# An S4D convolution beside a gated unit: magnitude powers two at a time over five chunks, output stores of the first half from GpSimd, the last Fourier stage before the last down block

## The chip, the cores and the metric

The kernel runs on one core of a Trainium2 chip. The core has five engines that work side by side, each in the order of its own instruction list: TensorE (matrix products), VectorE, ScalarE, GpSimd and SyncE, which only issues transfers. The metric is the device time of one execution in microseconds (us), lower is better; of several runs the median counts.

## What is computed

The layer norm of one input goes into two branches, and both are added to the input. Branch A is a state space convolution: a kernel of 2048 taps is generated for each of 448 channels from 256 complex modes, and convolved by Fourier transforms. Branch B is a gated unit with 1792 hidden columns.

```python
def _A_ref(u, log_A_real, A_imag, C_real, C_imag, log_dt, D_skip):   # u: (1, 2048, 448), modes: (448, 256)
    dt = jnp.exp(log_dt)
    A = -jnp.exp(log_A_real) + 1j * A_imag
    C = (C_real + 1j * C_imag) * dt[:, None]
    P = jnp.exp((A * dt[:, None])[:, :, None] * pos[None, None, :])
    K = 2.0 * jnp.einsum("dn,dnl->dl", C, P).real
    y = jnp.fft.irfft(Uf * Kf[None, :, :], L2)[:, :, :L]             # Uf, Kf: rfft of u and K at 2L
    y = y.transpose(0, 2, 1)
    return y + u * D_skip[None, None, :]

def _B_ref(x, w_gate, w_up, w_down):                                 # (448, 1792), (448, 1792), (1792, 448)
    h = _sigmoid(x @ w_gate) * (x @ w_up)
    return h @ w_down

xn = _layernorm(x)
return x + _A_ref(xn, ...) + _B_ref(xn, ...)
```

## The kernel before

Two Python generators, `conv` (branch A) and `glu` (branch B), emit instructions in turns; the main loop always continues the one that is behind by its planned share of work. A scheduler then sets the order within each engine's list, with `hp` (raised priority) and `issue_after` (not before a named instruction) as hints. At run time each engine works through its list in order and waits for semaphores.

**Branch A, generator `kgen`.** The 448 channels are worked in 56 chunks of 8 channels, 7 groups of 8 chunks. Per chunk TensorE multiplies phases by a selector (`tr`, line 539), ScalarE turns them into sines and cosines `S` (lines 545 to 548), VectorE multiplies those with magnitudes `me` and `mf` into `Et` and `Ft` (lines 599 to 601), and TensorE contracts them into `ko` (line 613). `S` for the next chunk is made one chunk ahead (`ahead`). The magnitudes are made by GpSimd for two chunks at a time (`magnitudes`, lines 505 and 517) by repeated doubling: each step multiplies a filled part of the row by one power. ScalarE adds squares to `me` (`squares`, line 530). GpSimd waits with a block until VectorE has read the block two before it, since `me` has two buffers.

**The powers.** `powers` makes what the doubling multiplies by: twelve arrays `pm[:, j]` for a whole group. It holds each power minus one, and VectorE squares it in that form (line 453: (w + 2) w), ten times in a chain; ScalarE adds the one at the end (line 451 for the first power, line 456 for j = 1 to 5 and for j = 7 to 11). `pm` has two buffers, one per group in turn. The first group's powers are made before the loop; those of group g + 1 are emitted at chunk 4 of group g (line 588), the magnitudes that read them at chunk 6. ScalarE's additions stand after `sins[0]`, the last sine step emitted so far.

**Branch B, `glu`.** Two halves of 1024 tokens. Per block of 128 hidden columns `gate` makes products `gu` (line 706), a tanh, and `hf`, the product of gate and up (line 717); its rounded part `hh` and rest `hl` feed the down products `po` (line 819) that VectorE adds into `acc` (line 824). Products are in split precision, three per pair.

**The end.** `spectra` multiplies the spectra (`there`, `back`) for the column half h = 0, then h = 1; `last(h, m)` is the closing Fourier stage (line 960) for four token blocks, two in each half of the tokens, and VectorE adds its result (line 968). The sums of tokens 0 to 1023 are in `ac`, the rest in `accs[2]` and `accs[3]`. `H` is 224, half the columns. `out` stores four token blocks of one column half in four transfers, which go to SyncE, ScalarE and GpSimd in rotation (`outs`). In the last group of `glu` (`final`) the down blocks run (t, b) = (0, 0) to (1, 3); before (1, 2) stand `last(1, 0)` and `last(1, 2)`, behind (1, 3) `last(1, 4)` and `last(1, 6)`. The first column half of `accs[2 + t]` is stored when block t is done, the second at the very end.

## Time and profile before

| | us |
|---|---|
| median of three runs | 716.96 |
| lowest, highest | 716.56, 721.07 |
| the profiled execution | 717.89 |
| its span in the profile | 716.1 |
| mean granted TensorE clock | 0.98 of full |

All durations come from the one profiled execution. A row of a timeline gives start, duration, engine, line, operation, output and inputs, shapes and count, and in brackets how long the engine stood idle before it and for whom. Rows that follow each other are merged, and "x6" says how many. A row of the groups gives the count, then busy time and mean of one in ns, then idle time before. A row of the waits gives who waited for whom: total, times, longest. PEld is TensorE's loading of weights, which runs beside the products; SPq and ACTq are the sequencers of SyncE and ScalarE issuing transfers.

### The profile page before, as it was taken

The page shows a single profiled execution, that of the slowest core. Times are in us where ns is not written, and L with a number is a line of the kernel's source. Part 1 is how long each engine was busy: PE and PEld are TensorE (multiplying, and loading weights), DVE is VectorE, ACT ScalarE, POOL GpSimd, SP SyncE. Part 2 cuts the span into 40 slices and gives each one's busy share as a digit, 9 for nine tenths or more (in the row PEclk, how much of TensorE's full clock was granted, in tenths as well). Part 3 has the DMA queues.
Part 4 walks back from the last instruction along what each step waited for, and adds up shares of the span by engine and source line. Part 5 has one row for each costly group of instructions (what it writes and reads, how often), then busy time and mean ns, then how long its engine had stood idle before and what let it go on. Part 6 is the DMA issues. An engine that isn't in the chain of part 4 may idle for free.

```text
span 716.1 us, 19096 instructions
## 1 busy us (share of the span) xinstructions
PE 671.3 (94%) x7752; PEld 528.2 (74%) x7752; DVE 550.8 (77%) x766; ACT 428.7 (60%) x678; POOL 378.8 (53%) x431
## 2 busy tenths in 40 slices
PE   3898999999997998999999999999989999999995
PEld 2676888878876885656878778887867777776784
DVE  5899997599889889898588988987936555556543
ACT  3656974588687689996578778678643322313320
POOL 2101138556987978797368688598954002351002
PEclk9998999999999898999999999999999999999998
DMA  9947174464254444556933333242259988999645
GB/s 204 235 145 231 50 230 132 145 198 136 63 169 148 138 111 127 160 164 196 274 107 101 95 110 116 68 147 57 57 173 309 242 234 239 264 281 222 182 131 154
DMA packets 93991, 117.22 MB, mean 164 GB/s; under 512 B 12240, under 2 KB 77776, under 8 KB 93904
## 3 DMA queue, kind: packets, MB, share of 16 engines
q1 hardware_dynamic: 65904, 91.87, 45.6%
q10 hardware_dynamic: 25424, 18.24, 8.8%
q0 software_dynamic: 2576, 5.90, 2.9%
q8 instruction: 61, 1.00, 0.6%
q14 instruction: 26, 0.21, 0.1%
HBM read 72.13 MB, written 43.84 MB: 162 GB/s over the span
## 4 chain that ended last, share of the span: by engine, by line
PE 71%; DVE 13%; ACT 4%; issue 3%; SPq 3%; DMA 3%; POOL 1%; ACTq 0%; POOLq 0%; DVEq 0%
PE gu L706 29%; PE po L819 17%; PE sp L900 7%; PE ko L613 6%; PE pv L927 4%; PE tr L539 4%; SPq L489 2%; DVE Et L599 1%; PE gu L281 1%; DVE Ft L601 1%; DVE Et L600 1%; DMA acc<-in_A_u_dram 1%; DMA ph<-ph_d 1%; DVE pm L453 1%; DVE hl L724 1%
## 5 line engine op out<-in xcount | busy, mean ns | idle before, releaser
L517 POOL TENSOR_TENSOR me<-me,pm 128x32 f32<-128x32 f32 (+1 forms) x168 | 145.1, 864 | 67.6 <-DVE Et L600 56.8
L517 POOL TENSOR_TENSOR mf<-mf,pm 128x64 f32<-128x64 f32 (+1 forms) x112 | 121.3, 1083 | 6.1
L706 PE MATMUL gu<-xh,wh 128*128 128x512 f32 x336 | 100.5, 406 | 0.7 <-ACT xh L221 0.7
L706 PE MATMUL gu<-xh,wl 128*128 128x512 f32 x336 | 96.2, 393 | 0.0
L706 PE MATMUL gu<-xl,wh 128*128 128x512 f32 x336 | 96.1, 392 | 0.0
L600 DVE TENSOR_TENSOR Et<-me,S 128x1024 f32<-128x1024 f32 x56 | 79.7, 1423 | 14.4 <-ACT me L530 14.0
L599 DVE TENSOR_TENSOR Et<-me,S 128x1024 f32<-128x1024 f32 x56 | 79.1, 1414 | 14.3 <-ACT S L548 13.6
L819 PE MATMUL po<-dh,hh 128*128 128x448 f32 x224 | 85.0, 379 | 2.9 <-DVE hf L717 2.9
L601 DVE TENSOR_TENSOR Ft<-mf,S 128x1024 f32<-128x1024 f32 x56 | 80.1, 1430 | 6.5 <-PE ko L613 4.0
L819 PE MATMUL po<-dl,hh 128*128 128x448 f32 x224 | 83.1, 371 | 0.0
L819 PE MATMUL po<-dh,hl 128*128 128x448 f32 x224 | 81.8, 369 | 0.0
L545 ACT ACTIVATE S<-tr 128x1024 f32<-128x1024 f32 x56 | 57.9, 1034 | 37.8 <-PE tr L539 36.1
L613 PEld LDWEIGHTS ko<-Et,Ft 128*32 128x32 f32 x3584 | 55.5, 112 | 30.6 <-issue 13.6
L706 PEld LDWEIGHTS gu<-xh,wh 128*128 128x128 f32 x336 | 61.7, 191 | 19.8 <-issue 4.4
L613 PE MATMUL ko<-Et,Ft 128*32 128x64 f32 x3584 | 66.5, 224 | 9.4 <-DVE Ft L601 7.4
L722 ACT CAST hh<-hf 128x512 fp32r<-128x512 f32 x56 | 35.0, 625 | 65.6 <-DVE hf L717 58.3
L706 PEld LDWEIGHTS gu<-xh,wl 128*128 128x128 f32 x336 | 63.4, 189 | 14.4 <-DVE hf L717 0.7
L706 PEld LDWEIGHTS gu<-xl,wh 128*128 128x128 f32 x336 | 63.4, 189 | 13.5
L783 POOL TENSOR_TENSOR dl<-rd,dh 128x448 fp32r<-128x448 f32 x14 | 26.2, 1871 | 83.5 <-ACT dh L782 83.5
L548 ACT ACTIVATE S<-S,hpi 128x1024 f32<-128x1024 f32 x56 | 65.7, 1174 | 0.0
L824 DVE SCALAR_TENSOR_TENSOR acc<-po,acc 128x448 f32<-128x448 f32 x80 | 48.0, 615 | 21.1 <-PE po L819 21.0
L717 DVE SCALAR_TENSOR_TENSOR hf<-th,gu 128x512 f32<-128x512 f32 x56 | 38.0, 679 | 32.1 <-PE gu L706 24.5
(208 smaller groups left out, 1302.1 us busy)
## 6 DMA issues: line engine op xcount, KB each, us to landing
sk_d<-sk ACTq DMA_DIRECT2D x14, 512.0 KB
sx<-x_d SPq DMA_DIRECT2D x32, 224.0 KB
skl<-sk_d SPq DMA_DIRECT2D x16, 448.0 KB
vp<-v_d SPq DMA_DIRECT2D x16, 448.0 KB
v_d<-vt SPq DMA_DIRECT2D x14, 448.0 KB
ph<-ph_d SPq DMA_DIRECT2D x224, 24.0 KB
wt_d<-wh SPq DMA_DIRECT2D x9, 512.0 KB
wt_d<-wl SPq DMA_DIRECT2D x9, 512.0 KB
```

The source lines that it names most:

```text
L517: ins = nc.gpsimd.tensor_tensor(m[:, :, w + a : 2 * w : n], m[:, :, a:w:n], par(base + i).unsqueeze(2).to_broadcast([128, 4 * DC, w // n]) ...
L545: nc.scalar.activation(rows(cs), pv, AF.Abs)
L548: sins[:] = [nc.scalar.activation(cs, cs, AF.Sin, scale=-TWO_PI, bias=hpi)]
L599: v.tensor_tensor(Et[:, :, :, 32:64], two(me[:, :, 32:64]), S[:, 1::-1], ALU.mult)
L600: v.tensor_tensor(Et[:, :, :, 0:32], two(me[:, :, 0:32]), S[:, 1:3, :, ::-1], ALU.mult)
L601: fts[:] = [v.tensor_tensor(Ft, two(mf), S[:, 3:5], ALU.mult)]
L613: mm = nc.tensor.matmul(ko[32 * j : 32 * j + 32, sl], Ft[:, cc, DC * h + 4 * q + j], Et[:, cc, DC * h + 4 * q + j], start=(k == 0), stop=( ...
L706: glu_mm[:] = [nc.tensor.matmul(ps, a_, b_, start=(n == 0), stop=(n == len(mm) - 1))]
L717: marks[1] = v.scalar_tensor_tensor(hf, th, 1.0, pgu[1], ALU.add, ALU.mult)
L819: glu_mm[:] = [nc.tensor.matmul(po, a_[:, bs], w_, start=(n == 0), stop=(n == 3 * fc - 1))]
L824: v.scalar_tensor_tensor(acc[:, b], po, 0.5, acc[:, b], ALU.mult, ALU.add)
L900: mm = nc.tensor.matmul(to, tb[:kk, t, 64 * c : 64 * c + 64], rhs, start=True, stop=True, skip_group_check=True,)
```

## The change

Three things are changed. First, `powers` takes a list of steps. `PWS` gives chunks 1 to 5 of each group two of the ten VectorE steps each (6 and 12 are passed over), and chunk 6 the three ScalarE additions, all in one place. The magnitudes of the next group are still emitted at chunk 6, after them. Second, `out` takes the engines, the blocks and the columns as arguments. The first column half of all tokens is stored by GpSimd alone, the rest by SyncE and ScalarE. Third, `last(1, 4)` and `last(1, 6)` now stand before the down block (1, 3), with the stores of all that is then ready; behind it only its own block is stored, with all columns.

```diff
+PWS = [(), (1, 2), (3, 4), (5, 7), (8, 9), (10, 11), (12,)]
...
-    def out(src, b0, h):
-
-        ds = slice(H * h, H * h + H)
+    def out(src, b0, nb, ds, engs):
+
         for g in range(4):
-            eng = (nc.sync, nc.scalar, nc.gpsimd)[outs[0] % 3]
-            outs[0] += 1
-            eng.dma_start(blocks(out_t, g, b0, 4)[:, :, ds], src[32 * g : 32 * g + 32, :, ds])
+            eng = engs[g % len(engs)]
+            eng.dma_start(blocks(out_t, g, b0, nb)[:, :, ds], src[32 * g : 32 * g + 32, b0 % 4 : b0 % 4 + nb, ds])
...
-    def powers(pms, g, behind=None):
+    def powers(pms, g, js=range(1, 13), behind=None):
...
-        with tc.issue_after(behind.ins) if behind else nullcontext():
-            nc.scalar.activation(pm[:, 0], w, AF.Identity, bias=one)
-        for j in (1, 2, 3, 4, 5, 7, 8, 9, 10, 11):
-            v.scalar_tensor_tensor(pm[:, j], w, 2.0, w, ALU.add, ALU.mult)
-            w = pm[:, j]
-        for o in (slice(1, 6), slice(7, 12)):
-            nc.scalar.activation(pm[:, o], pm[:, o], AF.Identity, bias=one)
+        for j in js:
+            if j in (6, 12):
+                continue
+            src = w if j == 1 else pm[:, j - 2 if j == 7 else j - 1]
+            v.scalar_tensor_tensor(pm[:, j], src, 2.0, src, ALU.add, ALU.mult)
+        if js[-1] == 12:
+            with tc.issue_after(behind.ins) if behind else nullcontext():
+                nc.scalar.activation(pm[:, 0], w, AF.Identity, bias=one)
+                for o in (slice(1, 6), slice(7, 12)):
+                    nc.scalar.activation(pm[:, o], pm[:, o], AF.Identity, bias=one)
...
-                if c == 4 and NCH * (g + 1) < NCK:
+                if 0 < c < 7 and NCH * (g + 1) < NCK:
                     with tc.issue_after(fts[0].ins):
-                        powers(pms, g + 1, sins[0])
+                        powers(pms, g + 1, PWS[c], sins[0])
...
-                        if final and (t, b) == (1, 2):
+                        if final and t == 1 and b >= 2:
 
                             sp_mm[:] = glu_mm
-                            for m in (0, 2):
+                            for m in (4 * b - 8, 4 * b - 6):
                                 lasts[0](1, m)
+                            if b == 3:
+                                out(accs[2], 8, 4, slice(H, D), (nc.sync, nc.scalar))
+                                out(accs[3], 12, 3, slice(0, D), (nc.sync, nc.scalar))
...
-                    if final:
-                        out(acc, 8 + 4 * t, 0)
-                if final:
-                    sp_mm[:] = glu_mm
-                    for m in (4, 6):
-                        lasts[0](1, m)
-                    for t in range(2):
-                        out(accs[2 + t], 8 + 4 * t, 1)
+                    if final and t == 0:
+                        out(acc, 8, 4, slice(0, H), (nc.gpsimd,))
+                    elif final:
+                        out(acc, 15, 1, slice(0, D), (nc.sync, nc.scalar))
...
-                    out(ac[:, 4 * q : 4 * q + 4], 4 * q, h)
+                    out(ac[:, 4 * q : 4 * q + 4], 4 * q, 4, ds, (nc.sync, nc.scalar) if h else (nc.gpsimd,))
```

Line numbers in the changed kernel lie one to five higher. The numbers behind tile names are those of buffers: `S_1107` and `S_1103` are the two buffers of S, `pm_1110` and `pm_1167` the two of the powers.

The first place is ScalarE's list in the second group, at the sines of chunk 12 (the first row) and chunk 13 (the last). Before:

```order
L548 ACTIVATE S_1107<-S_1107,hpi 128x2x512
L530 ACTIVATE me_1109<-me_1109 128x32x8
L451 ACTIVATE pm_1110<-W_108,one 128x128
L722 CAST hh<-hf 128x512
L714 ACTIVATE th<-gu 128x512
L456 ACTIVATE pm_1110<-pm_1110,one 128x640
L530 ACTIVATE me_1109<-me_1109 128x32x16
L456 ACTIVATE pm_1110<-pm_1110,one 128x640
L623 COPY ks<-ko 128x512
L545 ACTIVATE S_1103<-tr 128x2x2x256
```

The same place in the changed kernel, and then the place, two chunks on, where the additions now stand:

```order
L550 ACTIVATE S_1107<-S_1107,hpi 128x2x512
L532 ACTIVATE me_1109<-me_1109 128x32x8
L724 CAST hh<-hf 128x512
L532 ACTIVATE me_1109<-me_1109 128x32x16
L716 ACTIVATE th<-gu 128x512
L625 COPY ks<-ko 128x512
L547 ACTIVATE S_1103<-tr 128x2x2x256
```

```order
L550 ACTIVATE S_1107<-S_1107,hpi 128x2x512
L532 ACTIVATE me_1101<-me_1101 128x32x8
L456 ACTIVATE pm_1110<-W_108,one 128x128
L458 ACTIVATE pm_1110<-pm_1110,one 128x640 x2
L724 CAST hh<-hf 128x512
L532 ACTIVATE me_1101<-me_1101 128x32x16
```

The three additions have left the stretch between the sines of chunk 12 and chunk 13, and stand behind the sines of chunk 14.

The second place is VectorE's list in the third group, around the powers there. Before:

```order
L717 SCALAR_TENSOR_TENSOR hf<-th,gu 128x512
L601 TENSOR_TENSOR Ft<-mf_1102,S_1103 128x1024
L453 SCALAR_TENSOR_TENSOR pm_1167<-W_108 128x128
L724 TENSOR_TENSOR hl<-hf,hh 128x512
L453 SCALAR_TENSOR_TENSOR pm_1167<-pm_1167 128x128 x3
L600 TENSOR_TENSOR Et_1105<-me_1109,S_1107 128x32x32
L453 SCALAR_TENSOR_TENSOR pm_1167<-pm_1167 128x128 x4
L599 TENSOR_TENSOR Et_1105<-me_1109,S_1107 128x32x32
L453 SCALAR_TENSOR_TENSOR pm_1167<-pm_1167 128x128
L601 TENSOR_TENSOR Ft<-mf_1108,S_1107 128x1024
```

The same steps of the chunks now:

```order
L719 SCALAR_TENSOR_TENSOR hf<-th,gu 128x512
L603 TENSOR_TENSOR Ft<-mf_1102,S_1103 128x1024
L453 SCALAR_TENSOR_TENSOR pm_1167<-pm_1167 128x128
L726 TENSOR_TENSOR hl<-hf,hh 128x512
L453 SCALAR_TENSOR_TENSOR pm_1167<-pm_1167 128x128
L602 TENSOR_TENSOR Et_1105<-me_1109,S_1107 128x32x32
L601 TENSOR_TENSOR Et_1105<-me_1109,S_1107 128x32x32
L603 TENSOR_TENSOR Ft<-mf_1108,S_1107 128x1024
```

Of the nine powers between the two Ft two are left; the others have gone to the chunks before and behind.

The third place is the end of GpSimd's list. Before:

```order
L645 DMA rdw<-in_B_w_down_dram 128x448
L240 DMA out_dram<-ac 32x4x224 x2
L790 CAST dh<-rdw 128x448
L791 TENSOR_TENSOR dl<-rdw,dh 128x448
L240 DMA out_dram<-acc 32x4x224 x2
L240 DMA out_dram<-ac 32x4x224 x2
L240 DMA out_dram<-acc 32x4x224 x4
```

Now:

```order
L769 TENSOR_TENSOR wl<-wraw,wh 128x1024
L647 DMA rdw<-in_B_w_down_dram 128x448
L239 DMA out_dram<-ac 32x4x224 x8
L792 CAST dh<-rdw 128x448
L793 TENSOR_TENSOR dl<-rdw,dh 128x448
L239 DMA out_dram<-acc 32x4x224 x4
```

Eight stores of `ac` stand ahead of the last dh and dl instead of two, and behind them only the four of the first down block are left; six that stood at the end have gone to SyncE and ScalarE. On VectorE and TensorE the last two steps of the program change places: the four adds of line 968 now stand before the last add of line 824, and the closing products of line 960 before the last nine of line 819.

More of the change, by code (lines that the diff above doesn't have):

```diff
@@ L1106, in s4d_glu_kernel @@
     turns = []
-    lasts, glu_mm, sp_mm, glu_on, outs, x1s, hfs, xls = [], [], [], [], [0], [0], [], []
+    lasts, glu_mm, sp_mm, glu_on, x1s, hfs, xls = [], [], [], [], [0], [], []
     xq, psc, raws, acl, marks, slots, pqs = list(x_first), [], [], [], [None, None], {}, []
```

## The prediction

> **What bounds the kernel now.** I read the page's busy times first, then the windows of 75 us over the stretch in which the kernel generator and the gated unit run together, then the waits of TensorE and ScalarE, then the timeline at the two long stalls.

> ```profile
> span 716.1 us, 19096 instructions
> PE 671.3 (94%) x7752; PEld 528.2 (74%) x7752; DVE 550.8 (77%) x766; ACT 428.7 (60%) x678; POOL 378.8 (53%) x431
> ```

> TensorE is busy for 671.3 of 716.1 us, so there is little to win except its 45 us of idle time and time at a reduced clock. In the windows the columns are length, busy time of PE, PEld, DVE, ACT and POOL, then the granted clock.

> ```profile
> 150.00:225.00 75.00, 72.96 (x1088) 59.32 (x1086) 69.56 (x75) 57.55 (x84) 62.17 (x61) 1.00 0.41 125
> 225.00:300.00 75.00, 68.14 (x1038) 52.56 (x1038) 66.43 (x70) 61.96 (x94) 59.92 (x62) 0.91 0.50 150
> 300.00:375.00 75.00, 73.52 (x1023) 52.59 (x1027) 62.38 (x69) 56.12 (x90) 52.13 (x63) 1.00 0.61 181
> ```

> One window differs: 225 to 300 has 6.9 us idle, its neighbours 1.5 and 2.0, and only there is the clock below 1.00. Two TensorE stalls make it, and a stretch at half clock follows each (TensorE's timeline, then windows cut around them):

> ```profile
> 231.39 0.87 PE L613 MATMUL ko<-Et,Ft 128*32 128x64 f32 x24 [3.40 <-DVE Ft L601]
> 281.50 1.76 PE L281 MATMUL gu<-xt,wx 32*64 32x448 f32 x4 [2.81 <-DVE hf L717]
> 229.90:236.70 6.80, 5.31 (x108) 4.19 (x109) 6.43 (x7) 5.18 (x8) 6.57 (x7) 0.50 0.51 147
> 281.10:288.00 6.90, 6.50 (x84) 3.17 (x84) 6.40 (x9) 6.38 (x10) 4.38 (x7) 0.51 0.33 101
> ```

> **Part 1, the powers.** Today the ten power steps of a group stand in one run at chunk 4, six times after the first group. Their price on VectorE, and ScalarE's waits for them:

> ```profile
> L453 DVE SCALAR_TENSOR_TENSOR pm<-pm 128x128 f32<-128x128 f32 x63 | 32.5, 517 | 1.4
> L456 ACT ACTIVATE pm<-pm,one 128x640 f32<-128x640 f32 x14 | 11.7, 836 | 14.7 <-DVE pm L453 14.6
> L451 ACT ACTIVATE pm<-W,one 128x128 f32<-128x128 f32 x7 | 2.8, 406 | 0.0
> ```

> A run is 10 x 0.52 = 5.2 us of VectorE, and twice in it ScalarE, which works in order, stands before an addition of one until the power is there. Before the first stall its timeline reads:

> ```profile
> 216.97 0.83 ACT L456 ACTIVATE pm<-pm,one 128x640 f32<-128x640 f32 x1 [1.86 <-DVE pm L453]
> 217.71 0.65 ACT L530 ACTIVATE me<-me 128x512 f32<-128x512 f32 x1
> 220.49 0.83 ACT L456 ACTIVATE pm<-pm,one 128x640 f32<-128x640 f32 x1 [2.13 <-DVE pm L453]
> ```

> Behind the two waits, 1.86 + 2.13 = 4.0 us, stand in ScalarE's order a copy and the sines S of the next chunk (number 13, counted from 0). VectorE makes its Et and Ft from them:

> ```profile
> 226.23 1.22 DVE L599 TENSOR_TENSOR Et<-me,S 128x1024 f32<-128x1024 f32 x1
> ...
> 230.05 1.28 DVE L601 TENSOR_TENSOR Ft<-mf,S 128x1024 f32<-128x1024 f32 x1
> ```

> This Ft, done at 231.33, is what TensorE waits for. The 3.40 of that wait is less than the 4.0 that disappears. So I take this stall as gone, and with it half of TensorE's busy time at clock 0.50: 3.40 + 0.50 x 5.31 = 6.1 us. At the second stall the queue is VectorE's:

> ```profile
> 275.57 2.59 DVE L453 SCALAR_TENSOR_TENSOR pm<-pm 128x128 f32<-128x128 f32 x4
> 278.08 1.21 DVE L599 TENSOR_TENSOR Et<-me,S 128x1024 f32<-128x1024 f32 x1
> 279.21 0.50 DVE L453 SCALAR_TENSOR_TENSOR pm<-pm 128x128 f32<-128x128 f32 x1
> 279.64 1.21 DVE L601 TENSOR_TENSOR Ft<-mf,S 128x1024 f32<-128x1024 f32 x1
> 280.77 0.68 DVE L717 SCALAR_TENSOR_TENSOR hf<-th,gu 128x512 f32<-128x512 f32 x1
> ```

> The hf step must follow TensorE's last gu product, which ends where the stall begins (281.50 - 2.81 = 278.69), so its own 0.68 stays. Without the 2.59 + 0.50 of powers ahead, Et and Ft are done before that. The gain is 2.81 - 0.68 = 2.1, and of the clock 0.49 x 6.50 = 3.2: 5.3 us. Together 11.4. The powers' VectorE time itself neither grows nor shrinks: two per chunk, about 1.0 us, behind each Ft, in a VectorE that has 5 to 13 us free per 75.

> [...]

> What the change adds is lateness. The three additions now all come at chunk 6, behind the sines of chunk 6, and GpSimd's magnitudes of the next group, which read these powers, wait for them. In before they start as soon as Et of chunk 5 frees the buffer:

> ```profile
> 459.20 4.55 POOL L517 TENSOR_TENSOR me<-me,pm 128x32 f32<-128x32 f32 x5 [5.08 <-DVE Et L600]
> ...
> 465.06 2.05 POOL L517 TENSOR_TENSOR me<-me,pm 128x512 f32<-128x512 f32 x1
> 461.24 1.19 ACT L530 ACTIVATE me<-me 128x256 f32<-128x256 f32 x2
> 472.37 0.47 ACT L530 ACTIVATE me<-me 128x256 f32<-128x256 f32 x1
> ```

> By these rows the powers would be ready at 461.24 + 1.19 + 0.41 + 2 x 0.84 = 464.5, which is 5.3 us after 459.20, and the me chain would end at 467.1 + 5.3 = 472.4. The squares that read it run at 472.37. So the cover is used up, not exceeded: the cost per boundary is from nothing to 5.3 us. I take 0.7, since ko matrices stand some microseconds behind their Ft on TensorE and short lateness is mostly absorbed; six boundaries, 4.2 us. Part 1 is 11.4 - 4.2 = 7.2 us saved.

> **Part 2, the stores of the first column half.** ScalarE issues three of the eight stores between its compute steps:

> ```profile
> 638.93 5.27 ACTq L240 DMA_DIRECT2D out_dram<-ac  x3
> 644.25 0.60 ACT L714 ACTIVATE th<-gu 128x512 f32<-128x512 f32 x1 [9.21 <-DMA out_dram<-ac]
> 646.70 0.98 PE L900 MATMUL sp<-skl,tb 128*64 128x224 f32 x8 [0.30 <-ACT vt L933]
> 648.37 1.72 PE L960 MATMUL pv<-vp,wf 64*32 64x224 f32 x48
> 650.64 0.96 PE L960 MATMUL pv<-vp,wf 64*32 64x224 f32 x16 [0.55 <-DVE pd L912]
> ```

> The tanh waits behind them, and two TensorE gaps follow, 0.30 + 0.55 = 0.9 us, which I take as gone; if TensorE's slow pv products at 648.37 (1.72 + 0.96 against 1.74 at the end, below) have the same cause, another 0.9. GpSimd now issues eight, some 8 x 0.55 = 4.4 us, ahead of its last dh and dl. Those are read in the last down block, whose products stand at the end of part 3's rows, so they cost nothing as long as GpSimd has no other work there. SyncE too loses three stores from between its loads; no TensorE wait names a load here, so that counts as nothing, and the bound is the same 0.9 that I leave out.

> **Part 3, the end.**

> ```profile
> 705.72 1.74 PE L960 MATMUL pv<-vp,wf 64*32 64x224 f32 x64
> 706.47 3.56 SPq L240 DMA_DIRECT2D out_dram<-acc  x4
> 706.79 2.21 DVE L968 TENSOR_TENSOR acc<-acc,pv 128x448 f32<-128x448 f32 x4 [0.35 <-PE pv L960]
> 708.77 1.10 POOL L240 DMA_DIRECT2D out_dram<-acc  x2 [0.93 <-DVE acc L968]
> L1149 POOLq DRAIN  x3: 46/93/6027, 709.3 to 715.8; - x3
> L1149 SPq DRAIN  x3: 7/7/7, 713.9 to 715.6; - x3
> ```

> TensorE's end, 707.5, doesn't move, as the same products change places. After it stood 2.2 us of VectorE adds, stores until 710.0, and GpSimd's closing drain of 6.03 us, from 709.3 to 715.3. SyncE, which waits for the stores, was done at 713.9. So the drain costs 715.3 - 713.9 = 1.4. Afterwards one VectorE add, about 2.21 / 4 = 0.6, follows, then two short stores per queue. GpSimd's last store belongs to the first down block, four blocks of products before the end; if its drain keeps its 6.03 it is over before SyncE is done. The shorter adds save 2.21 - 0.6 = 1.6, but the stores left are many: four each of 32x4x224, 32x1344 and 32x448 floats, 112 + 168 + 56 KB, 1.3 MB in all. Half of the 1.6 I count as eaten by them. Together 1.4 + 0.7 = 2.1, between 0 (the stores end as late as now and a drain still ends last) and 1.4 + 1.6 + 0.5 = 3.5.

> **Sum.** The profiled execution took 717.89 us around its span of 716.1, 0.93 over the median of 716.96. 717.89 - 7.2 - 0.9 - 2.1 = 707.7, and as a median 706.8.

> **Rivals.**

> *The stalls come back elsewhere.* The static order of every engine is made anew, and a product put too early on TensorE waits as the two did. Against it: the other two windows quoted hold 1.5 and 2.0 us idle and no clock loss, though runs of powers stand in them too. The same rows speak for it: a run alone does not decide where a stall falls. Only parts 2 and 3 remain: 716.96 - 3.0 = 714.0.

> *GpSimd's late powers become the bound* (the slower side). It decides where a boundary's lateness passes what TensorE absorbs. If at three of six a stall like the first comes, 3.40 + 2.65, the 4.2 becomes 18.2: 706.8 + 14.0 = 720.8. For it: the zero cover above. Against it: GpSimd has 13 to 23 us free in each quoted window, and the me chain alone is early.

> *The pairs lengthen every chunk.* A power takes between 277 and 1171 ns:

> ```profile
> L453 DVE SCALAR_TENSOR_TENSOR pm<-pm x63: 277/400/1171, 107.3 to 451.0; 128x128 f32<-128x128 f32 x63
> ```

> If the spread ones all took the longest, 60 x 0.65 = 39 us more on VectorE, of which I let a quarter reach TensorE, the time would be 706.8 + 9.8 = 716.6. [...]

> *More is freed.* The 14.6 us of ScalarE waits were spread over all groups; without lateness and with the slow pv products gone, 706.8 - 4.2 - 0.9 = 701.7, or somewhat less.

> **Numbers.** Forecast 0.58, stalls elsewhere 0.20, late powers 0.10, longer pairs 0.05, more freed 0.07. The forecast's own range is 702 (no lateness) to 712.1 (the second stall's 5.3 stays). The range over the cases is 700 to 717; the late powers and a tail of the freed case lie outside. One per cent, 7.2 us, is about what a measurement of this kernel can tell from no change (the runs before lie between 716.56 and 721.07). Below 709.8 lie six sevenths of the forecast and the freed case, 0.57; within one per cent the rest of it, the stalls elsewhere, the long pairs and half of the late powers, 0.38; above, 0.05.

> **What would show it.** Right: no wait of ScalarE at its additions of one; window 225 to 300 at clock 1.00 and 2 us idle; TensorE no longer waiting for the Ft of chunk 13; tanh near 640 unblocked; GpSimd's drain over before SyncE's. Wrong: a stall of 2.8 us or more with half clock anywhere between 150 and 530, GpSimd's me step waiting for ScalarE's pm for over 5 us at each boundary, or a closing drain that still ends last.

## The result and the profile after

The changed kernel took 713.83 us in the median of 20 runs (711.26 to 717.94), the kernel before 719.06 in 20 runs beside them (715.23 to 725.74). The ratio is 0.9932, with a 95% interval from 0.9916 to 0.9949: about 4.9 us faster, where 10.2 were forecast. The profiled execution took 711.65 us around a span of 709.9, against 716.1 before. One execution among the experiments below, 756.73 us at a mean clock of 0.847 where the other eight of its kernel lie below 724, is in no figure. Lines 240 and 281 before are lines 239 and 280 now, one lower and not higher. The page's head:

```profile
span 709.9 us, 19096 instructions
PE 669.7 (94%) x7752; PEld 526.9 (74%) x7752; DVE 559.8 (79%) x766; ACT 428.8 (60%) x678; POOL 386.4 (54%) x433
```

TensorE's work has hardly changed; VectorE is 9.0 us busier with the same 766 instructions. The windows of 75 us (length, busy time of PE, PEld, DVE, ACT, POOL, then the granted clock):

```profile
150.00:225.00 75.00, 74.35 (x1092) 60.26 (x1091) 72.19 (x71) 60.17 (x86) 62.53 (x61) 1.00 0.43 135
225.00:300.00 75.00, 70.35 (x1133) 53.40 (x1131) 70.45 (x73) 63.75 (x99) 66.76 (x66) 0.95 0.49 143
300.00:375.00 75.00, 72.52 (x964) 53.44 (x960) 59.22 (x70) 52.90 (x83) 49.25 (x63) 0.95 0.59 178
```

The bad window from 225 to 300 is better than it was (0.95 for 0.91, 4.65 us idle for 6.9), but not clean. And the next one, which ran at 1.00 before, is now at 0.95 too. TensorE's timeline at the places where it waits there, idle time and releaser in brackets:

```profile
229.08 1.90 PE L615 MATMUL ko<-Et,Ft 128*32 128x64 f32 x64 [2.18 <-DVE Ft L603]
...
281.22 0.97 PE L280 MATMUL gu<-xt,wx 32*64 32x448 f32 x4 [1.25 <-DVE xl L220]
...
308.99 0.97 PE L280 MATMUL gu<-xt,wx 32*64 32x448 f32 x4 [0.91 <-DVE xl L220]
```

The wait for Ft of chunk 13 is 2.18 us, where it was 3.40. The second stall, 2.81, has become waits of 1.25 and 0.91 for xl, a step of VectorE that splits a transposed x block for the second half. Windows cut around these waits show the clock ahead of and behind each:

```profile
225.76:229.17 3.41, 1.23 (x20) 0.70 (x22) 3.41 (x4) 2.94 (x5) 3.15 (x3) 1.00 0.61 217
229.17:232.58 3.41, 3.41 (x86) 2.59 (x90) 3.41 (x4) 2.08 (x4) 3.33 (x5) 0.50 0.57 160
280.37:283.79 3.42, 2.57 (x12) 0.83 (x12) 3.42 (x5) 3.42 (x8) 3.42 (x3) 1.00 0.21 69
283.79:287.20 3.41, 3.06 (x69) 2.61 (x68) 2.44 (x3) 3.41 (x7) 3.25 (x6) 0.50 0.60 191
307.68:311.09 3.41, 2.50 (x36) 0.96 (x32) 3.41 (x6) 3.41 (x8) 3.16 (x6) 1.00 0.13 43
311.09:317.92 6.83, 6.58 (x59) 4.02 (x56) 6.76 (x9) 4.79 (x8) 6.46 (x6) 0.50 0.33 98
```

The half clock after the first wait is 3.41 us, not 6.8; but there is 3.41 after the second and 6.83 after the third. Between 220 and 330 us TensorE spends 13.65 us at half clock, and it spent 13.65 before (6.83 twice). In the rows ahead of the last two stretches TensorE was busy for 2.57 and 2.50 of 3.41 us. From 522.72 to 526.13 us of the same trace it was busy for only 1.63, and the clock stayed at 1.00 there and behind, so it was not idleness alone that took the clock.

ScalarE's queue did change as planned. Its additions of one (groups by line) wait 0.9 us in all, where they waited 14.7:

```profile
L458 ACT ACTIVATE pm<-pm,one 128x640 f32<-128x640 f32 x14 | 11.1, 836 | 0.9 <-DVE pm L453 0.9
```

The sines S of chunk 13 end at 220.4 us, 5.7 earlier than before (226.1). The Ft made from them ends only 2.3 earlier, for VectorE's timeline has this between the two:

```profile
219.75 1.35 DVE L453 SCALAR_TENSOR_TENSOR pm<-pm 128x128 f32<-128x128 f32 x2
221.03 0.67 DVE L719 SCALAR_TENSOR_TENSOR hf<-th,gu 128x512 f32<-128x512 f32 x1
221.63 1.49 DVE L601 TENSOR_TENSOR Et<-me,S 128x1024 f32<-128x1024 f32 x1
223.04 2.08 DVE L602 TENSOR_TENSOR Et<-me,S 128x1024 f32<-128x1024 f32 x1
225.05 1.22 DVE L762 TENSOR_TENSOR wl<-wraw,wh 128x1024 fp32r<-128x1024 f32 x1
226.19 1.62 DVE L726 TENSOR_TENSOR hl<-hf,hh 128x512 fp32r<-128x512 f32 x1
227.74 1.28 DVE L603 TENSOR_TENSOR Ft<-mf,S 128x1024 f32<-128x1024 f32 x1
```

There is no gap in it: VectorE's own queue is the next thing late. Then the stores and the end. ScalarE's tanh near 640 us, and the last rows of the timeline with the closing drains:

```profile
637.12 0.60 ACT L716 ACTIVATE th<-gu 128x512 f32<-128x512 f32 x1 [5.53 <-PE gu L708]
...
702.19 4.50 SPq L239 DMA_DIRECT2D out_dram<-acc  x6
702.20 4.51 ACTq L239 DMA_DIRECT2D out_dram<-acc  x6
...
703.20 0.62 DVE L829 SCALAR_TENSOR_TENSOR acc<-po,acc 128x448 f32<-128x448 f32 x1 [0.50 <-PE po L824]
...
L1150 POOLq DRAIN  x3: 46/93/5357, 694.4 to 709.6; - x3
L1150 SPq DRAIN  x3: 7/7/7, 709.0 to 709.4; - x3
```

The tanh waits for TensorE alone, not for stores. TensorE ends at 703.2, one add of 0.62 follows, and GpSimd's long drain begins at 694.4 and takes 5.36, so it is over before SyncE's at 709.0. From TensorE's end to the span's end it is 6.7 us, where it was 8.6.

### The profile page after: what moved, and what is told of

Same layout as the page of the kernel before. It is cut to its first block, busy times and chain, and to the rows that moved or that the text cites. A ratio compares the mean times of both kernels' runs of the same rounds, so it can differ in the third digit from the quotient of the medians.

```text
span 709.9 us, 19096 instructions
## 1 busy us (share of the span) xinstructions
PE 669.7 (94%) x7752; PEld 526.9 (74%) x7752; DVE 559.8 (79%) x766; ACT 428.8 (60%) x678; POOL 386.4 (54%) x433
## 4 chain that ended last, share of the span: by engine, by line
PE 68%; DVE 11%; DMA 7%; ACT 4%; SPq 3%; POOL 3%; issue 2%; ACTq 0%; DVEq 0%; POOLq 0%
PE gu L708 28%; PE po L824 15%; PE sp L901 7%; PE ko L615 6%; PE pv L928 4%; PE tr L541 4%; SPq L491 2%; DVE Ft L603 2%; POOL me L519 1%; DMA wraw<-in_B_w_gate_dram 1%; DVE Et L602 1%; PE pv L961 1%; DMA xe<-in_A_u_dram 1%; DVE Et L601 1%; DMA ph<-ph_d 1%
## 5 line engine op out<-in xcount | busy, mean ns | idle before, releaser
L519 POOL TENSOR_TENSOR me<-me,pm 128x32 f32<-128x32 f32 (+1 forms) x168 | 148.0, 881 | 61.5 <-DVE Et L602 34.1
L601 DVE TENSOR_TENSOR Et<-me,S 128x1024 f32<-128x1024 f32 x56 | 81.8, 1462 | 10.4 <-ACT S L550 8.8
L603 DVE TENSOR_TENSOR Ft<-mf,S 128x1024 f32<-128x1024 f32 x56 | 82.3, 1469 | 4.4 <-PE ko L615 2.3
L602 DVE TENSOR_TENSOR Et<-me,S 128x1024 f32<-128x1024 f32 x56 | 81.2, 1449 | 5.0 <-ACT me L532 4.6
L726 DVE TENSOR_TENSOR hl<-hf,hh 128x512 fp32r<-128x512 f32 x56 | 46.7, 833 | 18.6 <-ACT hh L724 14.1
```

Of the source, the lines that this page charges most:

```text
L519: ins = nc.gpsimd.tensor_tensor(m[:, :, w + a : 2 * w : n], m[:, :, a:w:n], par(base + i).unsqueeze(2).to_broadcast([128, 4 * DC, w // n]) ...
L601: v.tensor_tensor(Et[:, :, :, 32:64], two(me[:, :, 32:64]), S[:, 1::-1], ALU.mult)
L602: v.tensor_tensor(Et[:, :, :, 0:32], two(me[:, :, 0:32]), S[:, 1:3, :, ::-1], ALU.mult)
L603: fts[:] = [v.tensor_tensor(Ft, two(mf), S[:, 3:5], ALU.mult)]
L726: v.tensor_tensor(hl, hf, hh, ALU.subtract)
```

## The experiments

Two theories stood at first. A: part 1 removes waits, but stretches at half clock come back elsewhere and take the gain. B: GpSimd, which now gets the powers later, eats it.

**The parts by themselves.** Part 1 alone, in the kernel before, and parts 2 and 3 without part 1 (measured twice, the second time for the interval):

```diff
-                if c == 4 and NCH * (g + 1) < NCK:
+                if 0 < c < 7 and NCH * (g + 1) < NCK:
                     with tc.issue_after(fts[0].ins):
-                        powers(pms, g + 1, sins[0])
+                        powers(pms, g + 1, PWS[c], sins[0])
```

> The kernel before with the powers by twos alone (part 1); stores and end as before. The prediction's sum: 7.2 us below the kernel before. Theory A, the stalls and the half-clock stretches only move (the two traces show 13.6 us of half clock between 220 and 320 in both, and 4.5 us less idle time of TensorE): about 3 to 4 us below, ratio 0.995. Theory B, lateness of GpSimd at the group boundaries eats the gain: about the same 3 to 4 us, with waits of TensorE at the chunks that follow a boundary. It tells how much of the whole is part 1, not yet A from B.

> The changed kernel with the powers put back into one run at chunk 4: parts 2 and 3 alone. The prediction's sum: 0.9 + 2.1 = 3.0 us below the kernel before. By the milestones of the two traces (0.6 us between the end of the kernel generator and the end of the second half's last stage, 1.95 us behind TensorE's end): 2.5 us below. If part 1 gave nothing and all of the change's 5 us came from here: 5 below.

> The kernel with parts 2 and 3 alone once more, to set the interval of part 1. If part 1 is worth nothing on the mean (theory A: what it saves at full clock goes in half-clock stretches): 714 to 715, mean clock 0.985 to 0.986, full-clock span 702 to 703. If part 1 is worth 2 us or more: 716 or above.

Part 1 alone: 719.15 us against 718.85, ratio 0.9994 (0.9967 to 1.0022). Parts 2 and 3: 714.72, ratio 0.9931 (0.9904 to 0.9958), and the second time 715.44, 0.9955 (0.9929 to 0.9981). So nearly all of the gain is in parts 2 and 3, and part 1, for which 7.2 us were forecast, gives almost none (its interval allows at most 2.4). It is also less than the 3 to 4 us of theory A, whose figures were taken from two profiles. The profile of part 1 alone hides this too: at 715.77 us it is the third fastest of twelve runs between 713.73 and 723.80.

Every run has a span and a mean granted clock. Their product is called here the time at full clock, and the rest of the span the time lost to half clock (it also counts half clock while TensorE idles: at every profiled kernel's end, with TensorE done, stand 1.7 to 5.4 us of it, of which half is lost). Means over the runs, ± one standard error:

```
kernel                        runs  span     clock    at full clock   lost
before, beside experiments     91   717.1    0.9829   704.9 ± 0.2    12.2 ± 0.3
part 2 alone                   12   715.6    0.9829   703.4 ± 0.4    12.2 ± 0.7
part 3 alone                   12   715.1    0.9840   703.6 ± 0.4    11.4 ± 0.6
parts 2 and 3, both series     18   713.7    0.9842   702.4 ± 0.3    11.3 ± 0.5
part 1 alone                   12   716.7    0.9787   701.4 ± 0.7    15.3 ± 0.6
the changed kernel             20   712.4    0.9818   699.4 ± 0.3    13.0 ± 0.4
powers one chunk earlier        7   712.5    0.9834   700.7 ± 0.6    11.8 ± 0.7
powers of groups 2 to 6 out     6   710.5    0.9848   699.7 ± 0.6    10.8 ± 0.7
fillers in the second half's   12   713.5    0.9875   704.5 ± 0.4     8.9 ± 1.1
  first stage
powers clear of that stage     12   717.8    0.9800   703.5 ± 0.5    14.4 ± 0.6
```

Part 1 saves 3.5 us at full clock against the kernel before (704.9 to 701.4) and 3.0 when added to parts 2 and 3 (702.4 to 699.4). It loses 3.1 and 1.7 in half clock (12.2 to 15.3, 11.3 to 13.0). The net is 0.4 and 1.3 us, by mean spans with standard errors of 0.9 and 0.6: not told apart from nothing.

**Parts 2 and 3 apart.** The kernel before with one line for the stores (shown); and the changed kernel's end, with the powers in one run and the first half's stores dealt out as before:

```diff
             eng = (nc.sync, nc.scalar, nc.gpsimd)[outs[0] % 3]
             outs[0] += 1
+            if h == 0 and b0 < 12:
+                eng = nc.gpsimd
```

> The kernel before with the first half's twelve output stores on GpSimd (part 2) alone. The prediction: 0.9 us below the kernel before, 1.8 at most. Theory C, the stall behind ScalarE's stores near 640 us also takes the clock now and then (the trace of the powers-alone kernel has 3.41 us of half clock at 645 behind a stall of 2.06): 2 to 3 us below on the mean of the runs, and a mean clock 0.001 to 0.003 above the kernel before.

> The kernel before with the last Fourier stage ahead of the last down block and its stores on SyncE and ScalarE (part 3) alone; the first half's stores as before. The prediction: 2.1 us below the kernel before (0 to 3.5). With theory C true the two alone, 2.5 and 2, give the 4.1 that both together showed; with theory C false this one is 3.5 or more below.

Stores alone 717.56, ratio 0.9988 (0.9963 to 1.0013), 0.9 us; the end alone 716.80, ratio 0.9977 (0.9951 to 1.0004), 1.7 us. By mean spans they give 1.5 and 2.0, and together 3.4 (717.1 to 713.7). The prediction had 0.9 and 2.1. Each interval alone still holds no change; that of the two together does not. Theory C has no support: the clock with the stores alone, 0.9829, is that of the kernel before.

**Is GpSimd late?** Every pair of powers one chunk earlier; and the powers of five groups left out:

```diff
-PWS = [(), (1, 2), (3, 4), (5, 7), (8, 9), (10, 11), (12,)]
+PWS = [(1, 2), (3, 4), (5, 7), (8, 9), (10, 11), (12,)]
```

> The changed kernel with every pair of powers one chunk earlier, the additions of one at chunk 5 instead of 6; same work. Theory B (GpSimd gets the powers late, 0.7 us per boundary as the prediction charged, 4.2 in all): 3 to 4 us below the changed kernel, and GpSimd's waits for ScalarE's pm, 16 us in all in the changed kernel, mostly gone. Theory A: GpSimd's waits go too, but the time stays within 1.5 us of the changed kernel, with half-clock stretches at yet other places.

> Leaves out the powers of groups 2 to 6 (VectorE's steps and ScalarE's additions; GpSimd reads the powers of groups 0 and 1 again): the bound of what any placing of the powers can bring for those groups. Group 1's stay. Theory B and the theory that VectorE's own queue is the next late thing: at least 3 us below the changed kernel. Theory A: within 2 us of it, since only the clock's stretches decide and they come wherever a short stall falls.

GpSimd's first me step of a pair waits in the changed kernel, in its group of rows, 16.0 us for the additions; one chunk earlier it waits for Et alone. First the changed kernel, then the other:

```profile
L519 POOL TENSOR_TENSOR me<-me,pm 128x32 f32<-128x32 f32 x28 | 20.1, 716 | 50.2 <-DVE Et L602 34.1 <-ACT pm L456 16.0
```

```profile
L519 POOL TENSOR_TENSOR me<-me,pm 128x32 f32<-128x32 f32 x28 | 19.8, 706 | 59.7 <-DVE Et L602 59.6
```

The waits went, and the time stayed: 714.23 us, ratio 0.9935 (0.9910 to 0.9959), against 0.9932. Theory B falls. With the powers out the kernel took 712.35, ratio 0.9904 (0.9877 to 0.9932), within 2 us of the changed one as theory A has it. At full clock it is no faster (699.7 against 699.4): spread by twos, the powers cost nothing there. What is left of their price is clock, 13.0 against 10.8.

**What halves the clock?** Cut into stretches of 3.41 us along the grid on which its changes lie, the 15 traces hold 2,887 stretches at full clock between 20 and 698 us; 63 were followed by half clock. For each I added up TensorE's busy time:

```
                                        busy share   followed by half   kept
all products counted in full            under 0.45         45              0
                                        0.45 or more       18           2824
products of 32x64 counted at a quarter  under 0.47         60              4
                                        0.47 or more        3           2820
```

The weight and the border were fitted to these rows, so they describe, no more (a row or two move with how products that overlap are counted). The quarter is of use only where the small products of the second half's first Fourier stage (gu from xt and wx) run, between 275 and 330 us. There a wait of 0.91 us was followed by half clock. A count without a weight says the same: of the 180 stretches that were busy for 0.50 to 0.90, these products filled 0.32 or more in 18, and twelve of the 18 were followed by half clock, three of these busy for 0.85 to 0.88; of the other 162 none was (this border, too, is read off the rows).

The place on the grid matters too. In the trace of the stores alone TensorE waits for the Ft of chunk 13 as long as in the kernel before (3.39 us for 3.40), and the clock stays full, for there the wait falls into two stretches, each of which is busy for about half:

```profile
231.71 1.10 PE L615 MATMUL ko<-Et,Ft 128*32 128x64 f32 x64 [3.39 <-DVE Ft L603]
226.67:230.08 3.41, 1.64 (x30) 1.03 (x28) 3.41 (x3) 3.41 (x7) 2.12 (x2) 1.00 1.01 339
230.08:233.49 3.41, 1.78 (x70) 1.33 (x74) 3.41 (x5) 2.69 (x6) 3.17 (x4) 1.00 0.66 207
```

To move the clock, one full product of constants was put in front of each pair of small ones (shown), and in another kernel nine into the wait for chunk 13:

```diff
         for g in range(4):
+            nc.tensor.matmul(pss[g], sel[:, 0:128], sel, start=True, stop=True)
             x_first_stage(pss[g][:, :D], xns, g)
```

> Adds work that the output does not need: in front of each pair of small 32x64 products of the second half's first Fourier stage one full 128x512 product of constants into the same bank, overwritten by the pair; 16 in all, about 0.23 us each. Theory A (the clock is halved after a 3.41 us stretch with too little work in the array, and the small products count little): the half-clock stretches between 270 and 325 us go or become fewer, the mean clock rises by 0.004 to 0.007, and the time is 0 to 3 us below the changed kernel although TensorE does 3.7 us more work. Rival (only idle time halves the clock, a busy stretch never): the clock stays, and the time is 1 to 4 us above the changed kernel.

> Adds work that the output does not need: nine full 128x512 products of constants, some 2.1 us, into a bank that is overwritten, where TensorE waits 2.18 us for the Ft of chunk 13. Theory A: no half clock at 229 in the profiled run, mean clock up by 0.002, time 0 to 2 us below the changed kernel. Rival (the clock has nothing to do with it): nothing gained, or up to 1 us lost where the filler outlasts the wait.

With the fillers in that stage the mean clock rose from 0.9818 to 0.9875 and the loss fell by 4.0 us, although TensorE had more to do: the size that theory A named. The time did not fall, 715.89 us, ratio 0.9952 (0.9923 to 0.9982), 2.1 above the changed kernel where A said 0 to 3 below: 5.1 us came on top at full clock, of which 16 fillers at the 0.23 us estimated ahead are 3.7. The fillers also filled idle time (in the windows below TensorE is busy for 53.92 of 55 us, for 50.90 without them), so this run doesn't tell the small products from the waits; only the count above does. The windows over this stage, of the changed kernel, of parts 2 and 3 without part 1, and with the fillers:

```profile
275.00:292.00 17.00, 14.85 (x236) 9.23 (x234) 14.69 (x17) 16.27 (x28) 16.45 (x19) 0.90 0.49 152
292.00:330.00 38.00, 36.05 (x519) 22.77 (x516) 36.45 (x42) 33.10 (x53) 31.38 (x34) 0.91 0.47 152
```

```profile
275.00:292.00 17.00, 14.12 (x184) 8.80 (x174) 14.68 (x19) 14.31 (x24) 14.09 (x18) 0.80 0.39 125
292.00:330.00 38.00, 35.75 (x544) 21.84 (x544) 37.31 (x39) 35.43 (x60) 31.15 (x32) 1.00 0.50 162
```

```profile
275.00:292.00 17.00, 15.92 (x174) 8.96 (x173) 14.35 (x15) 15.42 (x26) 16.53 (x17) 0.80 0.44 139
292.00:330.00 38.00, 38.00 (x518) 23.17 (x519) 31.83 (x39) 30.96 (x51) 26.55 (x32) 1.00 0.48 155
```

Part 1 makes the first row better and the second worse. The profile of part 1 alone has 0.90 and 0.91 too, and in all five profiles with the run at chunk 4 the second row is at 1.00. From 275 to 330 us those five hold 3.41 to 10.24 us of half clock, 6.83 on the mean, and the two with part 1 hold 10.24 each. With the fillers the second row is at 1.00 and the first again at 0.80. The fillers at chunk 13 gave no answer: 719.27 us, ratio 1.0012 (0.9980 to 1.0043). The static order of all engines was made anew around them, and the wait they were to fill became two others, 0.96 us at 227.7 and 2.33 at 231.6.

**Fillers far from the change.** Twelve products of the identity meant for each of two early waits, and for the first alone:

```diff
+                    if gates[0] == 2 and i == 0 and n == 3:
+                        with tc.issue_after(glu_mm[0].ins):
+                            fill(trs[0][:, 1, :128])
                     glu_mm[:] = [nc.tensor.matmul(ps, a_, b_, start=(n == 0), stop=(n == len(mm) - 1))]
```

> The changed kernel with work added that the output does not need, in two waits of TensorE that have nothing to do with the change: twelve 128x128 products of the identity, some 2.5 us, in the wait of 2.76 us at 32.8 (xr) and twelve in the wait of 2.9 to 4.6 us at 60 (hf). Theory A (a 3.41 us stretch with too little work in it is followed by half clock, whatever the reason): the half-clock stretches near 35 and 62 go, 8.5 us of them on the mean of the ten profiles so far; full-clock time unchanged, mean clock up by 0.004 to 0.006, time 2 to 4 us below the changed kernel. Rival (the clock falls for another reason): clock unchanged, time equal or 0.5 us above.

> As the kernel with the two fillers, but with the first alone, in the wait at 32.8. Theory A: no half clock near 35 us, 3.4 us of it on the mean of the ten profiles, so mean clock up by 0.002 and 1 to 2 us below the changed kernel. Rival: nothing.

Both miss: 722.82 (1.0080, 1.0049 to 1.0111) and 723.98 (1.0081, 1.0061 to 1.0100), with mean clocks of 0.9827 and 0.9765. The first filler did what it should, 2.84 us in place of the wait, and no half clock stands near 35 us in either profile (it does in nine of the other thirteen, but not in that of the changed kernel, so this isn't shown to be the filler's work). The second did not land in its wait: it ran from 72.2 us, behind it, and the wait of 4.82 us at 60 and the half clock behind it stayed. And the order after the fillers was made anew: chunk 8 starts 7.0 and 7.9 us later than in the changed kernel. An edit that adds an instruction here is no clean test of its own price.

**Another place for the powers.** One run at chunk 2; and by threes and fours so that none falls into the stage at 275 to 325:

```diff
+PW2 = [(), (1, 2, 3, 4), (5, 7, 8), (9, 10, 11), (), (), (12,)]
+PW3 = [(), (), (), (1, 2, 3), (4, 5, 7, 8), (9, 10, 11), (12,)]
...
+                js = {2: PW2, 3: PW3}.get(g, PWS)[c] if c < 7 else ()
```

> The changed kernel with the ten powers of a group in one run again, but at chunk 2, the additions at chunk 6 as in the change: no wait of ScalarE for powers, no pair of powers in each chunk. Theory A (the weak stretches of the second half's first Fourier stage near 280 to 320 decide the clock, whoever delays them): the time stays within 2 us of the changed kernel. Rival D (pairs of powers in every chunk delay VectorE's steps for that stage, which is what lowers the clock by 0.004): mean clock 0.984 to 0.987 as with the run at chunk 4, and 2 to 3 us below the changed kernel.

> The changed kernel with the powers of two groups placed clear of the second half's first Fourier stage (some 275 to 325 us): the group in progress there ahead of it in chunks 1 to 3, the next one behind it in chunks 3 to 5, three or four powers to a chunk; all other groups by twos as in the change. Rival D, now by place (a pair of powers ahead of VectorE's xl steps makes the weak stretches at 280 and 307 that halve the clock): no half clock near 310, mean clock 0.984 to 0.987 and 2 to 3 us below the changed kernel. Theory A alone (the stage is weak whoever delays it): clock and time as the changed kernel, within 1 us.

The run at chunk 2 took 720.59 us in the median of eight runs, ratio 1.0030 (1.0000 to 1.0060), where theory A had it within 2 us of the changed kernel and D 2 to 3 below. Its mean clock, 0.9845, is as high as rival D said, but TensorE is idle more: it waits eight times for Ft, 8.2 us in all, where the changed kernel waits three times, 3.3 us. The powers clear of the stage took 719.51, ratio 1.0005 (0.9980 to 1.0030), against D's 2 to 3 us of gain. Its timeline and a window in the stage:

```profile
281.48 0.96 PE L282 MATMUL gu<-xt,wx 32*64 32x448 f32 x2 [1.70 <-DVE xl L222]
...
277.00:300.00 23.00, 21.24 (x238) 11.03 (x241) 14.12 (x15) 16.18 (x29) 12.10 (x15) 0.70 0.32 100
```

With no power near, TensorE waits 1.70 us for the same xl, and then runs at half clock for 13.65 us. Rival D falls: the stage was weak with no power ahead of xl too. Theory A's own figure, within 1 us of the changed kernel, is missed, as the time is 5.7 above it; 4.1 of that is time at full clock, which no run here explains. So A has the clock in part 1 right, but its forecasts of a time failed for part 1 alone, the fillers and both of these kernels. No version tried beats the changed kernel; only the one that leaves work out is below it.

## Why the prediction was half right

**The direction and parts 2 and 3 were right.** The tanh stands free, GpSimd's drain no longer ends last, and the two parts forecast at 3.0 us measure 3.4 by mean spans. Of part 3, the profiled time behind TensorE's end fell by 1.9 us for the 2.1 forecast.

**Part 1 was mis-sized: 7.2 us forecast, 0.4 to 1.3 measured.** Its mechanism was there, since the waits of ScalarE went. Term by term:

- *Half clock, the failed step.* Half of the busy time at clock 0.50, 2.65 + 3.2 = 5.9 us, was to be saved with the two stalls. It was not saved; 1.7 to 3.1 us more were lost. The step took the half clock for a fixed price of the one long stall ahead of it. It is no such price: in the five profiles with the run at chunk 4 the wait for the Ft of chunk 13 is 3.36 to 3.40 us, and the half clock behind it 6.83 in three, 3.41 in one and none in one. By the rows it belongs to a 3.41 us stretch with too little work in it, and between 275 and 330 us, among the small products, waits of 1.25 and 0.91 were followed by more of it than one of 2.81 was before. Which of the two counts how much is a fit and not shown.
- *The first stall* was taken as gone, since 3.40 is less than the 4.0 that ScalarE no longer waits. It went to 2.18, because VectorE's own queue stood behind. The question "what is late next" was asked of ScalarE and not of the engine between it and TensorE.
- *The second stall*, 2.1 forecast, became 0.55, 1.25 and 0.91: next to nothing saved there. Shorter waits that the prediction didn't list, 1.49 at 411 us and 1.09 at 492, went instead.
- *GpSimd's lateness* was charged at 4.2 and costs nothing that could be measured: taking its waits away leaves the time the same. Without that charge the 5.5 us of idle time stand against 3.0 to 3.5 measured at full clock; with it the prediction had 1.3 there, so this part came out better than forecast, and the half clock alone turned the sum.

**The rivals.** "The stalls come back elsewhere", 714.0 us with a chance of 0.20, is what happened, though by the clock more than by idle time. As a time it is within 0.2 us, by luck; as a change it is 1.9 short (3.0 for 4.9), since the median before was 716.96 in the three runs shown and 719.06 in the twenty beside the result. GpSimd as the bound and the longer pairs did not come. VectorE's powers did get a little dearer, 34.4 us for 32.5, and its Et, Ft and hl steps by 9.9 in all, but with 26.5 us of powers left out the time at full clock is the same, so this does not reach TensorE. Of the signs named ahead, the free additions, the tanh and the drain came; the window at clock 1.00 and the end of the wait for chunk 13 did not. None of the three signs of being wrong came either: the longest wait between 150 and 530 us is 2.18, GpSimd waits over 5 us for the powers once (7.45 at 173.6 us) and not at each boundary, and the drain is over early. A sign that names one long stall doesn't see several short ones.

**One profile was read as if it were the mean.** The profile before ran at a clock of 0.980; the mean of 91 runs is 0.983. Its 14.4 us lost to half clock are 2.2 more than the usual 12.2, so it showed more to be saved than there was.

## What to carry to other kernels

Price a stall and the half clock that follows it apart: the wait goes with its cause, and the clock went here by the whole 3.41 us stretch around the wait. All 45 stretches busy for under 0.45 were followed by half clock and 18 of the 2,842 others, three of them rich in small products and busy for 0.85 to 0.88. After a wait is removed, walk each queue between the freed engine and the bound one before calling a stall gone. Where time at half clock is part of the sum, take it from the mean clock of many runs, not from one profile.

## What the runs showed of the hardware

Single steps differ from run to run too. The same two profiles have this Et in VectorE's timeline at the second stall, behind the same run of powers:

```profile
277.70 1.21 DVE L598 TENSOR_TENSOR Et<-me,S 128x1024 f32<-128x1024 f32 x1
```

```profile
280.21 2.15 DVE L598 TENSOR_TENSOR Et<-me,S 128x1024 f32<-128x1024 f32 x1
```

The stall in which it stands was 2.81 us in one and 5.54 in the other. What made one of the two steps 0.94 us longer was not tried.
